# Where the third and fourth tile of the first expert's rows are turned

## The chip, the cores and the metric

The kernel runs on one core of a Trainium2 chip. A core has a matrix engine (TensorE, PE in the profile, with PEld for its weight loads), VectorE (DVE), ScalarE (ACT), GpSimd (POOL) and SyncE (SP), each with its own stream of instructions; DMA queues move data beside them. The metric is the device time of one execution in microseconds (us); the time of a kernel is the median of its runs. Names such as L1303 are lines of the kernel.

## The reference

Two layers, all in float32. First an attention with 4 batches, 8 heads, 768 tokens and head size 64, in which a token sees 8 global keys and the 96 keys up to itself. Its output, 3072 rows of 512, goes to a router: each row is given to the one of 8 experts whose embedding has the largest cosine with it, and is sent through that expert alone.

```
expert_idx = np.argmax(logits, axis=1)
for e in range(E):
    mask = expert_idx == e
    h = np.maximum(x[mask] @ w1[e], 0.0)        # w1[e]: 512 x 1024
    out[mask] = gate_w[mask, None] * (h @ w2[e])  # w2[e]: 1024 x 512
```

How many rows an expert gets depends on the data.

## The kernel before

**Attention** fills roughly the first 176 us. While it ends, the router writes for each row its number and gate to a list per expert in DRAM. The first 256 rows of expert 0 are taken early: they are gathered, turned and multiplied with expert 0's first weights before the lists are complete (L654 to L674). What remains of expert 0 and all rows of experts 1 to 7 come afterwards, in the loop at L1732.

**Widths.** An expert's rows are gathered in four tiles of 128 (512 at most). How many of them are real is known only on the chip. choose_widths (L1471) picks for each expert the smallest of a list of widths that holds its rows: for expert 0's remainder 128, 160, 192 and so on up to 512 (13 widths, L27), for the other experts 256 to 512. The products of an expert stand in a Switch with one arm for each width (L1375); PE and ACT, and from expert 1 on DVE too, jump to the arm that a register names. A hint about the jump is given ahead (give_hint, L1517); for expert 0 that is at L1716.

**Gathers.** gather_rows (L986) has POOL issue four indirect DMAs, one for each tile, into buffers xg (8 of them, so those of expert 0 are used again by expert 2). prepare (L1682) calls it one expert ahead.

**Turning.** The first products take the rows as columns of xT, so the gathered tiles (a row on each partition) must be transposed. turn_row (L1013) does that for one tile: four PE transposes into a PSUM tile "work" (three of them in turn), and two copies of 128x256 into xT, one for each half of the laced columns. The copies are done by the engine that is passed in.

```
for a in range(2):
    copy(out=xT[:, :, a, j * half : (j + 1) * half].rearrange(...), in_=laced(ps[:])[:, a])
```

xT holds all 512 columns, tile j in columns 64j to 64j+63 of each half. A product for width w reads columns 0 to w/2 - 1 of each half.

**Order around the change.** It is written by hand (a manual schedule on all engines); within one engine instructions run in the order of the program. From L1694 on:

- the lists' heads are loaded, cast to indices, and expert 0's four gathers are issued on POOL (L1706), then on SP the remaining pieces of expert 1's second weights, which wait for all four gathers (L1711 to L1714);
- pair.begin (L1718) multiplies the early 256 rows with the second weights, on PE;
- expert 0's four tiles are turned, with VectorE copying (L1721);
- VectorE casts the other experts' lists (L1723), splits them (L1724), clears the arms' result tiles (L1725) and makes sums of expert 1's first weights (L1728);
- the loop starts: POOL issues expert 1's gathers (L1739), and expert 0's Switch begins (L1375).

In an arm of expert 0, first_by_eight (L1273) multiplies the w columns of xT with the first weights in eight row blocks; ScalarE evicts each (L1281). After the row blocks 5, 6 and 7 the arm turns the tiles of expert 1 (between, L1355), with ScalarE copying. Then come the second products: part_in_arm (L1241) for a remainder of 32 or 64 rows and second_in_arm (L1232) for whole tiles beyond the first, and half of the first tile's product (L1390). Behind the arms follow the rest of it and the end of the early pair. At the loop's next turn POOL issues expert 2's gathers and then the scatters of expert 0's results (L1740); SP asks for expert 2's weights when the last of these scatters has landed (L1743).

For experts 1 to 7 the arms use first_by_seven (L1286), which saves one of eight block products by sums that VectorE makes; the tiles of an expert are turned in the arms of the expert ahead of it.

Of the kernel before, what the change touches and what calls it, by code (L numbers as in the profile page):

```python
# [20 lines left out]
P = 128  # L21
NEG = 1e9
CAP = 512
# [976 lines left out]
def new_turned(k):  # L1000
    return k.xtp.tile([P, k.NC, 2, CAP // 2], F32, name="xT", tag="xT")


def new_hidden(k):
    return k.hp.tile([P, k.NF, CAP], F32, name="hT", tag="hT")
# [80 lines left out]
def hidden_sums(k, a):  # L1086
    return left_sums(k, a, k.hsum)
# [258 lines left out]
def expert(k, now, coming, widths, unfinished):  # L1346


    tc = k.tc
    w1, w2 = now.w  # L1350
    hT = new_hidden(k)
    if coming:
        coming.xT = new_turned(k)

    def between(f):  # L1355
        at = {1: (0,), 2: (1,), 3: (2,), 4: (3,)} if now.e else {5: (0,), 6: (1, 2), 7: (3,)}
        for j in at.get(f, ()) if coming else ():
            turn_row(k, coming.rows, coming.xT, j, k.nc.scalar.copy)

    a = [[hT[:, 4 * j : 4 * j + 4, i * P : (i + 1) * P] for j in range(2)] for i in range(2)]  # L1360
    now.sums, spare = weight_sums(k, w2)
    left, making = hidden_sums(k, a)
    more, ahead = [], []
    if coming:
        coming.token_sums, more = token_sums(k, coming.xT)
        if now.e:
            coming.first_sums, ahead = first_sums(k, coming.w[0])
    spare = [spare[:2], spare[2:], ahead[:1], ahead[1:2], more[:2], []]
    if now.e == 1:
        spare[2:6] = [], ahead[:1], ahead[1:2] + more[:1], more[1:2]  # L1370
    tiles = range(2 if now.e else 1, CAP // P)
    ps = None if now.e else k.work0.tile([P, k.DM], F32, name="work", tag="work")
    k.order = list(range(4, 8)) + list(range(4)) if now.e else list(range(8))
    steps = widths_of(now.e)
    for arm in tc.Switch(now.width.index, len(steps), hint=now.width.hint):  # L1375
        w = steps[arm]
        if now.e:
            first_by_seven(k, now, hT, w, between, list(spare))
            for make in making:
                make()  # L1380
        else:
            first_by_eight(k, now.xT, w1, hT, w, between)
        for size in (32, 64):
            if w % (2 * size) >= size:
                part_in_arm(k, now, hT, w2, w // (2 * size) * 2 * size, size)
        for j in tiles:
            if j < w // P:
                second_in_arm(k, now, hT, w2, j)
        if ps:
            second(k, ps, hT, w2, range(k.NF // 2))  # L1390

    def scatters():
        for j in tiles:
            scatter_rows(k, now.y[:, j - 1, :], now.tile_ids[:, j : j + 1])
        for size in (64, 32):
            scatter_rows(k, now.y_part[size][:], now.parts[size][0], P // size)

    def choose_next():
        if coming:
            give_hint(k, coming.e, widths[coming.e])  # L1400

    out = [scatters]
    if now.e:
        pair = Pair(k, now.rows, a, left, w2, now.sums, not coming)
        choose_next()
        out += unfinished.pop()()
        number = [lambda: widths.append(take_width(k, now.e + 2))] if now.e + 2 < k.E else []
        if now.e == k.E - 2:
            number.append(lambda: load_flag(k))
        if now.e == 2:  # L1410
            ahead.append(lambda: flag_leftover(k))
        pair.begin(spare=(more[2:], number + ahead[2:3], ahead[3:]))
        ps = k.work0.tile([P, k.DM], F32, name="work", tag="work")
        unfinished.append(pair.end(ps[:, 0:256]))
        out.append(pair.scatter(1))
    else:
        choose_next()
        widths.append(take_width(k, 2))
        out += unfinished.pop()()
        for make in more:  # L1420
            make()
        second(k, ps, hT, w2, range(k.NF // 2, k.NF))
        unfinished.append(lambda: end_second(k, now.rows, ps))
    return out


def widths_of(e):
    return WIDTHS[PAIR:] if e else WIDTHS
# [168 lines left out]
def kernel(  # L1597
# [40 lines left out]
    with ExitStack() as moe:  # L1638
# [55 lines left out]
        with tc.manual_schedule(engines=ORDERED | set(ARMS) | {mybir.EngineType.Pool}):  # L1694
            choose_widths(n)
            sums, making = weight_sums(n, n.w[0][1])
            for make in making:
                make()
            numbers(0, 2)
            a = [[h[:, :, i * P : (i + 1) * P] for h in n.first.hT] for i in range(2)]  # L1700
            left, making = hidden_sums(n, a)
            making[1]()
            making[2]()
            making[0]()
            cast(0, 1)
            coming = prepare(0)  # L1706
            gathers = coming.gathers
            making[3]()
            cast(1, 2)
            numbers(2, n.E)  # L1710
            for e, i in n.weights:  # L1711
                part = load_weights_part(n, e, n.w[e], i)
                wait_for(n, part, gathers)
                gathers = []  # L1714
            widths = [take_width(n, 0), take_width(n, 1)]
            give_hint(n, 0, widths[0])  # L1716
            pair = Pair(n, n.first.rows, a, left, n.w[0][1], sums)
            pair.begin(True)  # L1718
            unfinished = [pair.end_apart]
            coming.xT = new_turned(n)  # L1720
            for j in range(CAP // P):  # L1721
                turn_row(n, coming.rows, coming.xT, j, nc.vector.tensor_copy)
            cast(2, n.E)  # L1723
            split_rows(n, n.mt)  # L1724
            for y, parts in ys:  # L1725
                for x in (y, *parts.values()):
                    nc.vector.memset(x[:], 0.0)
            first, making = first_sums(n, n.w[1][0])  # L1728
            for make in making:
                make()  # L1730
            pending = []
            for e in range(n.E):  # L1732
                now, coming = coming, None
                parts_of(n, now)
                now.width = widths[e]
                if e == 1:
                    now.first_sums = first
                if e + 1 < n.E:
                    coming = prepare(e + 1)  # L1739
                for scatter in pending:  # L1740
                    scatter()
                if e and coming:
                    wait_for(n, load_weights(n, e + 1, coming.w), [n.outs[-1] if e == 1 else n.out_again])  # L1743

                nc.gpsimd.drain()
                pending = expert(n, now, coming, widths, unfinished)
            for scatter in pending + unfinished.pop()():
                scatter()
# [31 lines left out]
```

## Time and profile before

| what | value |
|---|---|
| median of 3 runs | 523.97 us (522.73 to 524.47) |
| the profiled execution | 524.56 us |
| its span | 522.8 us |
| granted TensorE clock | 0.996 |
| PE idle between 200 us and its last matmul | 4.1 us in seven gaps over 0.1 us |
| expert 0's product, width 160 (L1279) | 209.75 to 220.0 us |

The profile is of one execution, and its span leaves out some 1.7 us around the program. In its timeline a line gives start, busy time, engine, line of the kernel, operation, tiles written and read, shape and number; in square brackets stands the idle time of that engine before it and what ended it. "issue" is time in which an engine waited for nothing that the profile shows. A chain of waits is followed back from the last instruction: at each step to what released it.

### The profile page before, as it was taken

The page shows a single profiled execution, that of the slowest core. Times are in us where ns is not written, and L with a number is a line of the kernel's source. Part 1 is how long each engine was busy: PE and PEld are TensorE (multiplying, and loading weights), DVE is VectorE, ACT ScalarE, POOL GpSimd, SP SyncE. Part 2 cuts the span into 40 slices and gives each one's busy share as a digit, 9 for nine tenths or more (in the row PEclk, how much of TensorE's full clock was granted, in tenths as well). Part 3 has the DMA queues.
Part 4 walks back from the last instruction along what each step waited for, and adds up shares of the span by engine and source line. Part 5 has one row for each costly group of instructions (what it writes and reads, how often), then busy time and mean ns, then how long its engine had stood idle before and what let it go on. Part 6 is the DMA issues. An engine that isn't in the chain of part 4 may idle for free.

```text
span 522.8 us, 13699 instructions
## 1 busy us (share of the span) xinstructions
PE 500.1 (96%) x5606; PEld 411.3 (79%) x5606; DVE 301.8 (58%) x602; ACT 197.2 (38%) x493; POOL 153.7 (29%) x169
## 2 busy tenths in 40 slices
PE   7899999999988998999999999999999999999995
PEld 7677887887765787859878759989889789859964
DVE  5647667666685664756745606765646644715531
ACT  4867766766653411302322312412312222302210
POOL 4221121442544235354240024144053050013023
PEclk9999999999998999999999999999999999999999
DMA  9999998898443346817573018357056064001001
GB/s 169 200 188 181 220 261 207 212 229 177 104 103 92 94 102 118 265 56 287 195 284 118 2 44 296 150 197 263 3 217 242 4 224 163 1 16 67 0 22 67
DMA packets 111421, 76.32 MB, mean 146 GB/s; under 512 B 87077, under 2 KB 95269, under 8 KB 111281
## 3 DMA queue, kind: packets, MB, share of 16 engines
q1 hardware_dynamic: 102769, 59.00, 42.1%
q0 software_dynamic: 6912, 15.26, 8.8%
q8 instruction: 63, 1.03, 0.9%
q14 instruction: 77, 0.63, 0.4%
q10 hardware_dynamic: 1600, 0.39, 0.3%
HBM read 61.66 MB, written 17.16 MB: 151 GB/s over the span
## 4 chain that ended last, share of the span: by engine, by line
PE 67%; issue 18%; DVE 3%; POOL 3%; ACT 3%; DMA 3%; SPq 1%; POOLq 1%; ACTq 0%; DVEq 0%
PE big L1303 17%; PE big L1108 9%; PE od L509 7%; PE pa L480 5%; PE work L1236 4%; PE od L519 3%; PE pa L455 3%; PE work L1108 3%; PE work L1249 3%; PE pa L671 2%; PE work L1017 2%; POOL out_dram L1255 2%; PE big L1279 2%; PE pa L582 2%; PE work L1027 1%
## 5 line engine op out<-in xcount | busy, mean ns | idle before, releaser
L493 DVE TENSOR_TENSOR ex<-ex,table 126x768 f32<-126x768 f32 x64 | 61.3, 964 | 45.1 <-ACT ex L486 44.9
L1315 DVE TENSOR_TENSOR hT<-big,hT 128x320 f32<-128x320 f32 (+4 forms) x70 | 39.4, 566 | 49.9 <-PE big L1303 49.7
L1255 POOL DMA_INDIRECT out_dram<-y_arm,tids x17 | 17.1, 1004 | 167.4 <-ACT y_arm L1238 121.1
L486 ACT ACTIVATE ex<-pa 126x384 f32<-126x384 f32 (+1 forms) x128 | 53.3, 477 | 24.4 <-PE pa L480 18.6
L1303 PE MATMUL big<-xT,w1t 128*128 128x160 f32 (+4 forms) x336 | 59.4, 330 | 1.1 <-issue 1.1
L1303 PEld LDWEIGHTS big<-xT,w1t 128*128 128x128 f32 x336 | 54.2, 190 | 3.9 <-issue 2.0
L991 POOL DMA_INDIRECT xg<-x_dram,idss x32 | 35.4, 1106 | 42.9 <-PE big L1303 21.5
L509 PE MATMUL od<-ex,v 126*64 126x192 f32 (+1 forms) x576 | 47.0, 309 | 0.0
L480 PE MATMUL pa<-qT,kT 64*32 64x128 f32 (+4 forms) x2048 | 41.0, 263 | 3.7 <-issue 3.5
L480 PEld LDWEIGHTS pa<-qT,kT 64*32 64x32 f32 (+1 forms) x2048 | 30.2, 105 | 16.7 <-issue 12.3
L257 POOL DMA_INDIRECT meta<-mt,slot x24 | 27.2, 1133 | 49.9 <-DVE rd L553 20.9
L509 PEld LDWEIGHTS od<-ex,v 126*64 126x64 f32 x576 | 35.3, 139 | 7.9 <-issue 3.8
L1303 PE MATMUL big<-xsum,fsum 128*128 128x160 f32 (+4 forms) x224 | 39.6, 330 | 0.0
L1020 ACT COPY xT<-work 128x256 f32<-128x256 f32 x56 | 18.1, 375 | 56.0 <-PE work L1017 55.3
L1303 PEld LDWEIGHTS big<-xsum,fsum 128*128 128x128 f32 x224 | 36.1, 190 | 1.2
L1236 PE MATMUL work<-w2t,hT 128*128 128x512 f32 x80 | 35.1, 594 | 0.0
L1108 PE MATMUL big<-wsum,hsum 128*128 128x256 f32 x136 | 31.1, 380 | 1.1 <-issue 0.6
L1317 ACT ACTIVATE hT<-hT 128x320 f32<-128x320 f32 (+4 forms) x42 | 21.6, 533 | 25.5 <-DVE hT L1315 25.3
L430 POOL COPY v<-v 30x896 f32<-30x896 f32 (+1 forms) x15 | 18.4, 1239 | 41.1 <-DMA v<-in_v_dram 28.9
L1108 PEld LDWEIGHTS big<-wsum,hsum 128*128 128x128 f32 x136 | 25.7, 190 | 5.6 <-issue 1.4
L1236 PEld LDWEIGHTS work<-w2t,hT 128*128 128x128 f32 x80 | 15.1, 190 | 17.7 <-issue 17.6
L1113 DVE TENSOR_TENSOR ptmp<-big,ptmp 128x256 f32<-128x256 f32 x16 | 6.7, 421 | 38.0 <-PE big L1108 20.0
(246 smaller groups left out, 899.8 us busy)
## 6 DMA issues: line engine op xcount, KB each, us to landing
w1t<-in_moe_w_dram SPq DMA_DIRECT2D x6, 2048.0 KB
w2t<-in_moe_w_dram SPq DMA_DIRECT2D x6, 2048.0 KB
v<-in_v_dram SPq DMA_DIRECT2D x32, 192.0 KB
x_dram<-xs SPq DMA_DIRECT2D x23, 256.0 KB
k<-in_k_dram SPq DMA_DIRECT2D x28, 192.0 KB
q<-in_q_dram SPq DMA_DIRECT2D x28, 192.0 KB
w1t<-in_moe_w_dram SPq DMA_DIRECT2D x32, 128.0 KB
w2t<-in_moe_w_dram SPq DMA_DIRECT2D x32, 128.0 KB
```

The lines of the kernel that those rows point to most:

```text
L257: i = nc.gpsimd.indirect_dma_start(out=k.meta[:], out_offset=bass.IndirectOffsetOnAxis(ap=slot[:, t : t + 1], axis=0), in_=mt[:, t, :], in ...
L480: i = nc.tensor.matmul(u.sp[e][k0:k1, a * n + c0 : a * n + c1], lhsT=t.kT[rows, j, k0:k1], rhs=t.qT[rows, j * BLK + c0 : j * BLK + c1], st ...
L486: nc.scalar.activation(u.ex[:, e], u.sp[e][0:ROWS, 0 : 2 * u.n].rearrange("p (a c) -> p a c", a=2), AF.Exp, scale=k.scale)
L493: nc.vector.tensor_tensor(out=exv, in0=exv, in1=tab[:, :, 0 : u.n // BLK, :], op=ALU.mult)
L509: nc.tensor.matmul(g.od[a][e * D : (e + 1) * D, at : at + c1 - c0], lhsT=g.v[0:ROWS, 2 * a + e, u.j, :], rhs=u.ex[:, e, a, c0:c1], start=f ...
L991: i = k.nc.gpsimd.indirect_dma_start(out=xg[:], out_offset=None, in_=k.x_dram[0 : upto or k.N + 1, :], in_offset=bass.IndirectOffsetOnAxis ...
L1108: i = self.k.nc.tensor.matmul(ps, lhsT=x[:, f, :], rhs=w[:, f, :], start=f == 0 and not add, stop=True, skip_group_check=True)
L1236: nc.tensor.matmul(ps[:], lhsT=hT[:, f, j * P : (j + 1) * P], rhs=w2[:, f, :], start=i == 0, stop=i == k.NF - 1)
L1255: i = k.nc.gpsimd.indirect_dma_start(out=k.out.rearrange("t (i m) -> (t i) m", i=n), out_offset=bass.IndirectOffsetOnAxis(ap=ids, axis=0), ...
L1303: nc.tensor.matmul(to[f // 2][:, f % 2 * 256 : f % 2 * 256 + h], lhsT=x[:, l, f * P : (f + 1) * P], rhs=y[:, l, 0:h], start=not (add or f ...
L1315: nc.vector.tensor_tensor(out=to, in0=x, in1=z, op=ALU.add)
L1317: nc.scalar.activation(to, to, AF.Relu)
```

## The change

Ahead of expert 0's Switch only the first two tiles are turned. In an arm, ahead of its products, those further tiles are turned that this arm's width reaches: none for widths up to 256, the third for 288 to 384, the third and fourth for 416 to 512. There ScalarE copies them, where VectorE did before. For the other experts turned_ahead gives 4, so the new loop has no turns. All four gathers are issued as before.

```diff
     for arm in tc.Switch(now.width.index, len(steps), hint=now.width.hint):
         w = steps[arm]
+        for j in range(turned_ahead(now.e), -(-w // P)):
+            turn_row(k, now.rows, now.xT, j, k.nc.scalar.copy)
         if now.e:
...
+def turned_ahead(e):
+    return CAP // P if e else 2
...
             coming.xT = new_turned(n)
-            for j in range(CAP // P):
+            for j in range(turned_ahead(0)):
                 turn_row(n, coming.rows, coming.xT, j, nc.vector.tensor_copy)
             cast(2, n.E)
```

## The prediction

> **What bounds the kernel now.** I read the page's busy shares and its chain first, then the chain and the timeline around the changed lines.
>
> ```profile
> PE 500.1 (96%) x5606; PEld 411.3 (79%) x5606; DVE 301.8 (58%) x602; ACT 197.2 (38%) x493; POOL 153.7 (29%) x169
> PE 67%; issue 18%; DVE 3%; POOL 3%; ACT 3%; DMA 3%; SPq 1%; POOLq 1%; ACTq 0%; DVEq 0%
> ```
>
> TensorE is the bound: 96% busy, and 67% of the chain. "DMA 3%" is small, but one piece of it lies exactly where the change works. The chain between 204 and 222 us:
>
> ```profile
> 204.00 4.61 DMA xg<-x_dram,idss
> 208.60 0.14 issue
> 208.74 0.63 PE work L1017 x4
> 209.36 0.39 issue
> 209.75 6.76 PE big L1279 x48
> ```
>
> Columns: start, duration, what. The gather of the fourth tile of expert 0's rows is issued at 204.00 and ends 4.61 us later. TensorE waits for it, turns that tile (four transposes, L1017), and only then begins expert 0's first product (L1279). The timeline of the same stretch, start and busy time first:
>
> ```profile
> 204.00 0.95 POOL L991 DMA_INDIRECT xg<-x_dram,idss  x1 [0.30 <-issue]
> 206.13 1.47 PE L1017 MATMUL work<-ident,xg 128*128 128x128 f32 x12
> 206.80 1.41 DVE L1020 COPY xT<-work 128x256 f32<-128x256 f32 x4
> 208.74 0.63 PE L1017 MATMUL work<-ident,xg 128*128 128x128 f32 x4 [1.13 <-DMA xg<-x_dram,idss]
> 209.75 6.76 PE L1279 MATMUL big<-xT,w1t 128*128 128x160 f32 x48 [0.39 <-issue]
> 210.02 0.76 DVE L1020 COPY xT<-work 128x256 f32<-128x256 f32 x2 [1.81 <-PE work L1017]
> 211.51 0.76 DVE L1020 COPY xT<-work 128x256 f32<-128x256 f32 x2 [0.73 <-PE big L1279]
> ```
>
> Twelve transposes (tiles 0 to 2) run without a gap, then TensorE idles 1.13 us for the DMA. The product's shape 128x160 tells which arm runs: width 160, which reads 160 columns, tiles 0 and 1 and no others. The last two rows are VectorE's copies of tiles 2 and 3; they start after the product has begun, so the product does not even wait for them.
>
> **The change part by part.** For width 160 the new loop in the arm is range(2, 2), so it is empty. In this run the work on tiles 2 and 3 is not moved, it disappears: eight transposes on PE, four copies on DVE.
>
> *PE, removed.* The third burst of four is a third of the run from 206.13 to 207.60: transposes start every 0.109 us, so 0.44 us. Then the wait, 1.13 us, and the last four transposes, 0.63 us. The 0.39 us of issue is the way into the Switch and stays. From the end of tile 1's transposes, 207.60 - 0.44 = 207.16, to the first product at 209.75 are 2.59 us.
>
> *What is late next.* The product needs both of tile 1's copies. They are in the row at 206.80: four copies in 1.41 us, to 208.21. I take 0.14 us from such an event to the first matmul (208.60 to 208.74 after the DMA): 208.21 + 0.14 = 208.35. The way into the Switch, 207.16 + 0.39 = 207.55, is hidden beneath the copies, with 0.80 us to spare. So the product starts at 208.35 and not at 209.75: **1.40 us earlier**. That is more than the bare wait of 1.13 and less than the 2.59 removed, because DVE's copies become the wait. Bounds: 2.20 us if the copies were not waited for (excluded: 32 columns of tile 1 are read), 0 if the wait for DVE took 1.40 longer than I think.
>
> *DVE.* Four copies at 0.417 us, 1.7 us, go, and the cast behind them (212.18) can start up to 4 us sooner. That is worth nothing on the path: the last of DVE's work there, expert 1's first sums (220.4 to 225.3), is read only from 237.1 on.
>
> *What must come as much earlier as PE.* The arm turns expert 1's rows after its sixth product; those transposes would move from 216.35, 217.88 and 219.84 to some 215.0, 216.5 and 218.4. The gathers for them are issued at 205.25 to 209.02; with the 4.61 us that expert 0's last gather took, the last lands at about 213.6. Cover: 4.8 us. ScalarE's evictions (L1281, 0.30 us each against 1.09 us of PE per row block) follow PE. From 235.3 on, stages show PE busy 32.86 of 34.00 and 247.66 of 248.70 us, so a shift at 210 us reaches the end; each expert's weights are released by PE's own progress (SP waits 137.5 us in five waits for "PE big L1108"), so the loads move with it.
>
> *Queues passed.* The gathers of tiles 2 and 3 are still issued, and the weight pieces on SP still wait for all four gathers: nothing moves there. POOL's gathers of expert 2 reuse the buffers of expert 0's tiles; for tiles 2 and 3 their last reader is now inside arms, some of which do not read them. The trace of before has no such release for these two. Lowest cost 0 (released at the arm's first instruction or before), highest as in the rival below. I take 0: these gathers start at 219.60, ten microseconds after the arm begins.
>
> *Code.* Eight transposes leave the common stream; eight wide arms that do not run here grow by four or eight transposes. Later code moves to other addresses. What a branch costs:
>
> ```profile
> L1775 PEldq COMPARE_BRANCH  x16: 295/314/3807, 209.0 to 499.3; - x16
> ```
>
> [...] Nearly all of it hides under matmuls already queued. The idle time of PE put to "issue" at the expert's ends is 0.55 us before L1108 at 228.15 and 1.14 us before L1303 at 269.27; the others are 0.3 us. Placing the code anew could remove these two (1.69 us) or lay bare a similar one elsewhere (+1.14). I take 0 for it, the trace having no sign which way.
>
> [...]
>
> *Sum.* 0.44 + 1.13 + 0.63 - 0.80 (new wait for the copies) = 1.40 us. The profiled execution took 524.56 us with a span of 522.8: the rest, 1.7 us, lies around it and stays, so it would take 523.16. The median of the runs is 0.59 below the profiled one; the same saving gives 523.97 - 1.40 = **522.6 us**.
>
> **The rivals.**
>
> *Faster still: code falls better.* The wait goes as above and the two bare "issue" gaps shrink as well. For it: they are tied to this layout. Against: nothing aims at them. 523.97 - 1.40 - 1.69 = 520.9 us.
>
> *No gain to speak of: a new wait in the old one's place.* PE now depends on a chain PE, DVE, PE just ahead of the product. The rows at 210.02 and 211.51 show that DVE may start late: tile 2's transposes ended at 207.60, and its copies started 2.4 us after that. Had tile 1's copies met such a delay, the product would start at 209.75 or later. Against: tiles 0 and 1 were copied without any gap. [...] 523.97 - 1.40 + 1.14 = 523.7 us.
>
> *Slower: the buffers come free too late.* If POOL may reuse the buffers of tiles 2 and 3 only when PE has left the arm and ended a product behind it (229.9 - 1.4 = 228.5), two gathers at 1.26 us come there, and POOL's scatters of expert 0's rows, begun now at 225.32, begin at 231.0 instead of 223.9: 7.1 us later. Expert 2's weights wait for the last of them (SP's longest wait for out_dram<-y,ids, 19.9 us), so they are asked for at 243.6 instead of 236.5. w1's 2.1 MB at the stage's 247 GB/s are 8.5 us, to 252; DVE reads them at 247.9 - 1.4 = 246.5, and behind that read stand the combinations that free PE's banks. PE would lose some 5 us less the 1.4 gained: 523.97 + 3.6 = 527.6 us. It decides only if the third gather waits more than 5 us: POOL idles 3.0 us between its gathers (end 222.35) and the first scatter, and the weights have about 2 us more. A branch into the arm that takes 3.4 us and no longer 0.39 (207.16 + 3.8 = 210.9) would also end above, at 525.1; but its hint is given at 195.0, 12 us ahead.
>
> *It does not do what it says* would be an arm other than 160; the shape 128x160 excludes that.
>
> **How the numbers follow.** Plain gain 0.62, better code 0.16, gain eaten 0.14, slower 0.08. About 0.3% (1.57 us) is what a measurement of this kernel can tell from no change. The plain gain, 1.40 us, lies just below it; with the small gaps of code and the scatter of the runs (522.73 to 524.47) I put 0.28 of its 0.62 beyond. Faster 0.28 + 0.16 = 0.44; same 0.34 + 0.14 = 0.48; slower 0.08. The range reaches from the better code (520.9) past the eaten gain (523.7) to the highest run shown, 524.5; the slower case and the tails stay out.
>
> **What would show it.** In the changed profile: eight transposes ahead of the product in place of sixteen, no wait for xg there, the product at about 208.35, DVE's copies at L1020 four in place of eight, L1279 again 128x160, the gathers of expert 2 near 218, the last pieces of the chain 1.4 us earlier. Wrong is the step on copies if the product starts behind 208.6; wrong is the step on the shift if the product starts at 208.35 and PE's last matmul does not end 1.4 us earlier; then the PE gaps at the joins tell where it went.

## The result, and the profile after

The kernel after took 525.68 us (median of 20 runs, 522.70 to 528.53). The kernel before, run beside it, took 526.41 us in 20 runs (522.11 to 529.37). The ratio is 0.9991, with an interval of 0.9971 to 1.0011: no difference that these runs can tell. The forecast, 522.6 us in a range of 520.9 to 524.5, lies 3.1 us too low. A few executions in the sets below were over 1.5% longer than the fastest of their kernel; the ratios and the differences at equal clock leave them out, the medians do not.

The first two lines are the busy times and the chain's shares on the page of the profiled execution of after (524.9 us, span 523.2).

```profile
PE 499.7 (96%) x5598; PEld 411.2 (79%) x5598; DVE 299.7 (57%) x598; ACT 197.0 (38%) x493; POOL 149.2 (29%) x169
PE 73%; issue 17%; ACT 4%; DVE 3%; POOL 2%; DMA 1%; POOLq 0%; DVEq 0%; ACTq 0%
```

Eight matmuls and four VectorE operations are gone, and the chain's DMA share fell from 3% to 1%. The chain of waits in the same stretch as before (start, duration, what):

```profile
203.79 4.75 PE big L1108 x22
208.54 0.89 PE work L1017 x8
209.43 0.02 issue
209.45 0.77 DVE xT L1020 x2
210.21 1.60 issue
211.81 6.76 PE big L1279 x48
```

No gather stands in it any more. In its place stand VectorE's copies and 1.60 us of "issue". The timeline (start, busy time, engine, line, operation; in brackets the idle time ahead) shows what that is:

```profile
208.38 1.04 PE L1017 MATMUL work<-ident,xg 128*128 128x128 f32 x8
209.45 0.76 DVE L1020 COPY xT<-work 128x256 f32<-128x256 f32 x2 [0.32 <-PE work L1017]
210.91 0.76 DVE L1020 COPY xT<-work 128x256 f32<-128x256 f32 x2 [0.70 <-PE work L1017]
211.81 6.76 PE L1279 MATMUL big<-xT,w1t 128*128 128x160 f32 x48 [2.40 <-issue]
```

TensorE ends the eight transposes at 209.42. VectorE is free at 210.21, yet it begins tile 1's copies only at 210.91: it is waiting for TensorE's signal that tile 1's transposes are done, and that signal comes 1.5 us after their end. (The ends of matmuls are modelled, so the profile cannot tell a late signal from transposes that really ended late; below both are called a late signal.) TensorE idles 2.40 us ahead of the first product. Before, it idled 1.52 us in two gaps and turned the two other tiles in the rest of that time.

**Where the time went, over all profiles.** The runs below gave several profiles of both kernels. I cut each at four points of the timeline: the first transpose of expert 0 (L1017), the first product of expert 0 (L1279), the first product of expert 1 (L1303's first), and the end of TensorE's last matmul. Times in us; an asterisk marks a stage in which TensorE ran at half clock for 3.41 us, which lengthens the first product by 1.7.

| profile | first transpose at | transpose to product | product to expert 1 | expert 1 to the end | gap before L1303 at expert 2 |
|---|---|---|---|---|---|
| before | 206.13 | 3.62 | 25.35 | 282.13 | 1.14 |
| before, e1 | 209.90 | 3.85 | 24.90 | 281.70 | 1.25 |
| before, e9 | 207.86 | 3.78 | 26.48* | 282.18 | 1.41 |
| after | 208.38 | 3.44 | 25.72 | 280.20 | none |
| after, e2 | 204.60 | 3.33 | 25.16 | 280.20 | none |
| after, e10 | 208.01 | 4.16 | 25.52* | 280.20 | none |
| after, e13 | 207.45 | 4.16 | 25.28* | 281.60 | 1.13 |

Three things can be read from it. At the place of the change nothing was gained on average: 3.75 us before (mean of three), 3.77 after (mean of four). Behind it, from expert 1 on, after is 1.45 us shorter on average (282.00 against 280.55), and that is the gap before L1303 at the way into expert 2's arm. And the start of the stage, in the second column, scatters over several microseconds, through code that is the same in both kernels. The fourth column differs by less than its scatter (means 25.58 and 25.42).

That gap in the timelines of before and then of after, TensorE alone:

```profile
266.24 1.89 PE L1108 MATMUL work<-w2t,hsum 128*128 128x256 f32 x8
269.27 3.04 PE L1303 MATMUL big<-xT,w1t 128*128 128x256 f32 x13 [1.14 <-issue]
```

```profile
268.66 1.89 PE L1108 MATMUL work<-w2t,hsum 128*128 128x256 f32 x8
270.39 1.89 PE L1303 MATMUL big<-xT,w1t 128*128 128x256 f32 x8
```

In the first, TensorE has nothing for 1.14 us; in the second, L1303 follows L1108 at once (consecutive groups overlap in these modelled ends). The branch ahead of it took 3397 ns in before and 404 ns in after.

### The profile page after: what moved, and what is told of

It reads as the page before. It is cut to its first block, busy times and chain, and to the rows that moved or that the text cites. A ratio compares the mean times of both kernels' runs of the same rounds, so it can differ in the third digit from the quotient of the medians.

```text
span 523.2 us, 13675 instructions
## 1 busy us (share of the span) xinstructions
PE 499.7 (96%) x5598; PEld 411.2 (79%) x5598; DVE 299.7 (57%) x598; ACT 197.0 (38%) x493; POOL 149.2 (29%) x169
## 4 chain that ended last, share of the span: by engine, by line
PE 73%; issue 17%; ACT 4%; DVE 3%; POOL 2%; DMA 1%; POOLq 0%; DVEq 0%; ACTq 0%
PE big L1303 17%; PE big L1108 11%; PE od L509 8%; PE pa L480 6%; PE work L1236 4%; PE od L519 4%; PE pa L455 3%; PE work L1108 3%; PE work L1249 3%; PE pa L671 3%; PE work L1017 2%; PE pa L582 2%; ACT ex L486 2%; POOL out_dram L1255 2%; PE big L1279 2%
## 5 line engine op out<-in xcount | busy, mean ns | idle before, releaser
L1303 PE MATMUL big<-xT,w1t 128*128 128x160 f32 (+4 forms) x336 | 59.3, 330 | 0.0
L1303 PEld LDWEIGHTS big<-xT,w1t 128*128 128x128 f32 x336 | 54.3, 190 | 2.4 <-issue 0.5
L480 PE MATMUL pa<-qT,kT 64*32 64x128 f32 (+4 forms) x2048 | 42.5, 263 | 5.7 <-issue 5.5
L991 POOL DMA_INDIRECT xg<-x_dram,idss x32 | 34.2, 1068 | 45.0 <-PE big L1303 19.2
L257 POOL DMA_INDIRECT meta<-mt,slot x24 | 26.1, 1087 | 49.6 <-DVE xs L591 10.5
L1303 PE MATMUL big<-xsum,fsum 128*128 128x160 f32 (+4 forms) x224 | 39.6, 330 | 0.0
L1303 PEld LDWEIGHTS big<-xsum,fsum 128*128 128x128 f32 x224 | 36.1, 190 | 1.2
L1108 PE MATMUL big<-wsum,hsum 128*128 128x256 f32 x136 | 31.1, 380 | 1.4 <-issue 0.9
L1108 PEld LDWEIGHTS big<-wsum,hsum 128*128 128x128 f32 x136 | 25.7, 190 | 6.0 <-issue 1.7
```

The costliest lines, as they stand in the source:

```text
L257: i = nc.gpsimd.indirect_dma_start(out=k.meta[:], out_offset=bass.IndirectOffsetOnAxis(ap=slot[:, t : t + 1], axis=0), in_=mt[:, t, :], in ...
L480: i = nc.tensor.matmul(u.sp[e][k0:k1, a * n + c0 : a * n + c1], lhsT=t.kT[rows, j, k0:k1], rhs=t.qT[rows, j * BLK + c0 : j * BLK + c1], st ...
L991: i = k.nc.gpsimd.indirect_dma_start(out=xg[:], out_offset=None, in_=k.x_dram[0 : upto or k.N + 1, :], in_offset=bass.IndirectOffsetOnAxis ...
L1108: i = self.k.nc.tensor.matmul(ps, lhsT=x[:, f, :], rhs=w[:, f, :], start=f == 0 and not add, stop=True, skip_group_check=True)
L1303: nc.tensor.matmul(to[f // 2][:, f % 2 * 256 : f % 2 * 256 + h], lhsT=x[:, l, f * P : (f + 1) * P], rhs=y[:, l, 0:h], start=not (add or f ...
```

## The experiments

Eighteen runs were made, in four sets; some repeat a kernel. Each set ran beside the kernel before on one chip: e1 to e4 on one, e5 to e8 on another, e9 to e12 on a third, e13 to e18 on that of e5 again at a later time (e16 to e18 eight minutes after e13 to e15, with no profile of after beside them). **Equal clock** below means this: each run lists its mean granted TensorE clock, and in every set the time falls as the clock rises, by 0.34 to 0.56 us per 0.001 (520 us times 0.001 is 0.52). One slope in common for a set, fitted by least squares over its runs, takes that part out; what is left of the difference to before is given with its standard error. The clock is itself a result of a run, so the ratio as measured stands beside it.

### First set: is it noise, and what holds the copies back?

**e1**, the kernel before as it is.

> The kernel before, unchanged, for the noise of times and the spread of single profiles. Read are three stretches: the start up to the first transpose of expert 0's rows (206.13 us in the profile of before, 208.38 in that of after, though the code up to there is the same), from the first transpose to the first product of expert 0 (3.62 before, 3.43 after), and from that product to TensorE's last matmul (307.49 before, 305.92 after). Theory S (the first stretch scatters by itself): it moves by 1 us or more against 206.13 here too, while the second stays within 0.2 of 3.62. Rival (a kernel's stages are fixed, so the 2.25 us of the first stretch are the change's own): 206.1 within 0.3. Ratio 1.000 with an interval of about 0.2% either way.

Measured: 525.88 us, ratio 0.9998 (0.9971 to 1.0025); at equal clock -0.16 +- 0.44 us.

**e2**, the kernel after as it is.

> The changed kernel, unchanged. Theory L (TensorE's last completion signals ahead of the jump into the arm reach VectorE late, so that the copies of tile 1 end some 3.3 us after the first transpose and the new wait eats the gain): first transpose to first product again 3.2 to 3.6 us. Rival A (that profile was an accident): 2.2 us, as predicted. Third stretch 305.9 again if it belongs to the layout of the code, 307.5 if the 1.6 us are scatter. Ratio 0.997 to 1.001.

Measured: 524.10 us, ratio 0.9967 (0.9937 to 0.9998); at equal clock -2.82 +- 0.45 us. The first product came 3.33 us after the first transpose: tile 1's copies were late again, by as much as in the first profile of after.

**e3**, three tiles turned ahead.

```diff
 def turned_ahead(e):
-    return CAP // P if e else 2
+    return CAP // P if e else 3
```

> Three tiles are turned ahead of the Switch, the fourth in the arms that read it, so there is no wait for the fourth gather, and tile 2's transposes stand between tile 1's and the jump. Theory L (the signals just ahead of the jump are late, whichever tile they belong to): the copies of tiles 0 and 1 come on time, as in the kernel before, and the first product starts 2.2 to 2.4 us after the first transpose; tile 2's copies come late and nobody waits. Rival T (the signals are late at this time because of the traffic of the gathers, wherever the jump is): 3.2 to 3.6 us, as in the changed kernel. Time under L 1.2 us less than before (ratio 0.998), under T as the changed kernel.

Measured: 523.59 us, ratio 0.9946 (0.9916 to 0.9976), at equal clock -1.92 +- 0.44. Tile 1's copies began 2.37 us after the first transpose although four more transposes stood behind tile 1's, and the product came at 3.27. So in this profile the signal is not late because a jump follows it: that theory falls. The gap before L1303 was there, 1.15 us.

**e4**, VectorE and ScalarE take one of each tile's two copies.

```diff
-def turn_row(k, rows, xT, j, copy):
+def turn_row(k, rows, xT, j, copy, other=None):
...
-        copy(out=xT[...
+        (other if a and other else copy)(out=xT[...
...
-                turn_row(n, coming.rows, coming.xT, j, nc.vector.tensor_copy)
+                turn_row(n, coming.rows, coming.xT, j, nc.vector.tensor_copy, nc.scalar.copy)
```

> The changed kernel, with each tile's second copy done by ScalarE, idle there, in place of VectorE, so that both copies of a tile run side by side. Theory L (the late signal is the wait): tile 1's signal comes 2.5 us after the first transpose as in the changed kernel, one copy of 0.4 us in place of two in a row of 0.77 behind it, and the product starts at about 3.1 us. If the copies' own length is the wait (the prediction's step): 1.04 for the transposes, 0.42 for the copies and 0.14, so 1.6 us. Time 0.3 to 0.4 us less than the changed kernel under L, 0.6 less under the other.

Measured: 523.14 us, ratio 0.9946 (0.9918 to 0.9974), at equal clock -2.65 +- 0.46. Product at 2.00, where theory L had 3.1 and the other 1.6: the signal of tile 1 was on time in this profile (VectorE began its copy at 1.07), but ScalarE's copies waited for VectorE's and the last began at 1.53. Gap before L1303: 1.09 us.

What follows: in this set the kernels with fewer turns ahead are some 2 to 3 us faster at equal clock (e2, e3, e4 against e1), though the first 20 runs of either kernel showed no difference; and in e2 and e3 the gain does not lie where the forecast had it.

### Second set: the code, and the traffic

**e5**, no executed instruction changed, only addresses. To the kernel before, the wide arms of expert 0 get the turns that the change puts there; all four tiles are still turned ahead.

```diff
         w = steps[arm]
+        for j in range(CAP // P if now.e else 2, -(-w // P)):
+            turn_row(k, now.rows, now.xT, j, k.nc.scalar.copy)
```

> The kernel before, with all four tiles turned ahead as it had them; only the wide arms, which do not run here, get the turns of tiles 2 and 3 that the change puts there (written a second time, to no effect). So no executed instruction differs from the kernel before, only the addresses behind the first expert's arms move. Theory K (the 1.14 us gap of PE before L1303 and its 3.2 to 3.6 us branch are a matter of where the code lies): the stretch from the first product to PE's last matmul leaves the 306.6 to 307.5 us of the two profiles of before, and if the gap happens to close it is 305.4 to 305.9, with a branch of about 0.4 us there; if the address falls badly too, it is unchanged or another gap shows. Rival N (the gap closed because the product began earlier, or because VectorE and POOL had less to do): gap of 1.1 us and 306.6 to 307.5, as before. Both: 3.6 to 3.9 us from the first transpose to the first product.

Measured: 519.86 us beside 519.80, ratio 0.9995 (0.9965 to 1.0025), at equal clock -0.18 +- 0.46. The gap before L1303 is gone and its branch took 409 ns. But the way out of expert 1's arm, where before, e1 and e9 show no gap, now shows one:

```profile
251.79 1.13 PE L1108 MATMUL big<-w2t,hT 128*128 128x256 f32 x4
253.94 1.02 PE L1108 MATMUL big<-w2t,hT 128*128 128x256 f32 x4 [1.01 <-issue]
```

So in this profile, with only the addresses moved, one gap is closed and another of nearly the same size stands elsewhere. Net: nothing.

**e6**, the kernel after without the turns in the wide arms.

```diff
-        for j in range(turned_ahead(now.e), -(-w // P)):
-            turn_row(k, now.rows, now.xT, j, k.nc.scalar.copy)
```

> The kernel after without the turns of tiles 2 and 3 in the wide arms (left out: what those arms would turn; the arm that runs here reads neither tile). Every executed instruction is that of the kernel after, the code behind the first expert lies lower. Theory K: the gap of 1.1 us before L1303 can come back, with a branch of 3.2 to 3.6 us, and the stretch from the first product to PE's last matmul goes from 305.4-305.9 back to about 307. Rival N: no gap, 305.4 to 305.9 as after. Both: 3.3 to 3.5 us from the first transpose to the first product.

Measured: 514.94 us beside 519.80 (six runs), ratio 0.9907 (0.9878 to 0.9936), at equal clock -3.64 +- 0.61. No gap before L1303, against what theory K allowed. And here is the forecast's own stretch as the forecast had it:

```profile
200.75 1.04 PE L1017 MATMUL work<-ident,xg 128*128 128x128 f32 x8
201.42 1.40 DVE L1020 COPY xT<-work 128x256 f32<-128x256 f32 x4
202.97 1.32 PE L1279 MATMUL big<-xT,w1t 128*128 128x160 f32 x8 [1.19 <-DVE idss L1684]
```

The four copies run on without a gap, and the product comes 202.97 - 200.75 = 2.22 us after the first transpose. The forecast had 208.35 - 206.13 = 2.22. The stretch ahead of it executes what after executes; only TensorE's signals came on time. (The release is put down to a later VectorE operation, the cast at L1684; it is the copies' end, 202.82, that the product waited for.)

**e7**, no gather in flight while tiles 0 and 1 are turned.

```diff
-            xgs, t.gathers = gather_rows(n, n.ids[:, e], n.xgp)
+            xgs, t.gathers = gather_rows(n, n.ids[:, e], n.xgp, CAP // P if e else 2)
+            if e == 1:
+                for x in t.gathers:
+                    wait_for_it(n, x, turned[-1])
+            xgs = xgs if e else xgs * 2
...
-                wait_for(n, part, gathers)
+                wait_for(n, part, turned[-1:])
```

> The kernel after with no gather in flight while the first two tiles are turned: the first expert's third and fourth gather are left out (their rows are never read here), and the second expert's four gathers and the pieces of its weights wait for VectorE's copy of the second tile. Theory T (TensorE's signals come late while gathers are under way): tile 1's copies start 1.05 to 1.4 us after the first transpose and the first product 2.0 to 2.3 us after it. Rival P (the lateness belongs to TensorE's own stream at this place, whatever the traffic): copies at 2.4 us, product at 3.3 to 3.5. The whole time will be longer in both cases, since the second expert's rows and weights are asked for later.

Measured: one run, 518.37 us. Product at 2.23. It tells nothing by itself, since e5, e6 and e8 had their signals on time too in this set.

**e8**, e3 and e4 together.

> Three tiles turned ahead, and each tile's two copies shared by VectorE and ScalarE. Theory S2 (two engines halve the copies; the signal's lateness is a matter of luck): the first product comes 2.0 to 3.0 us after the first transpose, 0.4 us below what one engine gives with the same signals; a signal at 2.4 gives copies to 2.85 and the product at 3.0. Rival (two waiting engines get the signal on time): 2.0 us again, as in the run with two tiles and two copiers. Time: 0.3 to 1.3 us below the kernel after if its code has no bare wait, and as much as 1.1 more with it.

Measured: 516.59 us beside 519.80, ratio 0.9951 (0.9928 to 0.9973), at equal clock -2.11 +- 0.47. Product at 2.00, gap before L1303 1.53 us.

### Third set: before and after side by side, once more

**e9**, **e10**, **e11** and **e12** are the kernels of e1, e2, e6 and e4 again.

> The kernel before, once more, for a profile of it on the same chip as the three runs that follow, and for the noise. Two theories of what the change brings meet here. Theory 1 (the sum of the forecast, 1.40 us at the way into the first product, plus 1.1 us for the bare wait before L1303): this profile shows 3.6 to 3.9 us from the first transpose to the first product and a gap of 1.0 to 1.25 us before L1303. Against the kernel before: 0, within 0.7 us.

Measured: 527.05 us, ratio 1.0000 (0.9971 to 1.0029), at equal clock -0.25 +- 0.47. Product at 3.78, gap 1.41.

> The kernel after, once more, beside before on the same chip. Theory 1: if tile 1's copies start on time (about 1.1 to 1.35 us after the first transpose, as in the run of the kernel without the arms' turns), the first product comes 2.2 us after the first transpose, 1.4 to 1.6 less than before; with the late start seen twice (2.4 to 2.5) it comes at 3.3 to 3.45. No gap before L1303. So at equal granted clock it is 2.5 to 3 us faster with signals on time, 1.5 to 2 with late ones. Rival 2 (the change is worth nothing): 0, within 0.7 us at equal clock.

Measured: 527.24 us, ratio 0.9988 (0.9951 to 1.0024), at equal clock -2.33 +- 0.50. Product at 4.16: later than in any profile of before. No gap before L1303. Rival 2 falls at equal clock, but not in the ratio as measured: the runs of after had a lower mean clock, 0.9918 against 0.9950 (in the first set 0.9954 against 0.9965).

The profile of e10 (mean clock 0.993) shows a stretch of lower clock. Busy time by windows of its timeline: length, then PE, PEld, DVE, ACT, POOL, then PE's granted clock, the DMA share and GB/s.

```profile
208.00:212.10 4.10, 1.05 (x9) 0.80 (x7) 2.08 (x7) 0.00 (x0) 2.91 (x4) 1.00 0.79 231
212.10:216.10 4.00, 3.94 (x17) 3.97 (x18) 3.53 (x24) 0.30 (x1) 0.00 (x0) 0.57 0.85 240
216.10:220.00 3.90, 3.90 (x31) 3.90 (x30) 3.29 (x5) 1.21 (x4) 0.60 (x1) 1.00 0.85 266
```

TensorE is nearly idle up to 212.1 and then has only 0.57 of its clock for 4 us: 17 matmuls where the next window of nearly the same length has 31. In the records of the clock this is one window of 3.41 us at half clock, and the product's 48 matmuls take 8.43 us and not 6.76.

> The kernel after without the turns in the wide arms (left out: what those arms, which do not run here, would turn), once more. Before, it stood 4.9 us below the kernel before in its six undisturbed runs. Theory 1: it executes what the kernel after executes, so at equal granted clock it stands with the kernel after within 0.7 us, unless a bare code wait differs, and each such wait is seen in its profile. Rival 3 (leaving out the arms' turns is worth something by itself, about 1 us or more): it is faster than the kernel after though no PE gap differs.

Measured: 526.31 us, ratio 0.9985 (0.9950 to 1.0021), at equal clock -2.59 +- 0.51, so with after (-2.33): rival 3 falls. Product at 3.44 this time, with a half-clock window behind it. No gap before L1303. The profile of e6 had signals on time, no half-clock window and no gap before L1303 (the bare code wait of the expectation) together; that these three made up its 4.9 us is likely, but no run took them apart.

> The kernel after with each tile's two copies shared by VectorE and ScalarE, once more. On-time signals: first product 2.0 us after the first transpose, only 0.2 less than with one engine; late signals: 2.8 to 3.0. Its bare wait before L1303 (1.09 us) stays, since the code lies as it did: so it is 0.5 to 1 us slower than the kernel after, at equal clock, with signals on time, and about equal with late ones.

Measured: 524.78 us, ratio 0.9960 (0.9932 to 0.9987), at equal clock -3.53 +- 0.47. Product at 2.06, and no gap before L1303 (branch 403 ns), though the code is that of e4, which had 1.09. So the addresses within the program do not settle the gap alone. The expectation that it would be slower than after is refuted. Its stretch, with one of tile 1's copies on each engine:

```profile
205.82 1.04 PE L1017 MATMUL work<-ident,xg 128*128 128x128 f32 x8
206.50 0.88 DVE L1020 COPY xT<-work 128x256 f32<-128x256 f32 x2
206.94 0.84 ACT L1020 COPY xT<-work 128x256 f32<-128x256 f32 x2 [1.68 <-DVE xT L1020]
207.88 1.32 PE L1279 MATMUL big<-xT,w1t 128*128 128x160 f32 x8 [1.02 <-DVE xT L1020]
```

### Fourth set: one cause or two, and where the lateness comes from

**e13** is the kernel after, **e14** and **e16** that of e7, one run each.

> The kernel after, for its profile beside the next two on one chip. With late signals: tile 1's copies 2.4 to 3.3 us after the first transpose, first product at 3.3 to 4.2. With signals on time: copies at 1.3, product at 2.2. No gap before L1303 in both cases.

Measured: 525.98 us; product at 4.16. Contrary to the expectation the gap before L1303 was there, 1.13 us, with a branch of 3293 ns: the kernel after can meet it too.

> The kernel after with no gather in flight while tiles 0 and 1 are turned (the first expert's third and fourth gather left out, the second expert's gathers and weight pieces held until the copies of tile 1), once more. If the kernel after shows late signals in this same job: theory T (the gathers make TensorE's signals late) expects copies of tile 1 at 1.05 to 1.4 us and the first product at 2.0 to 2.3; rival P (the lateness has another source) expects 2.4 or later, and 3.3 or later. If the kernel after shows none, this run tells nothing on that.

Measured: 523.76 us; product at 2.23, in the same set in which after had 4.16.

**e15**, the kernel before without the wait for the third and fourth gather.

```diff
             coming.xT = new_turned(n)
+            first_two = (None, None, coming.rows[2][:2] * 2)
             for j in range(CAP // P):
-                turn_row(n, coming.rows, coming.xT, j, nc.vector.tensor_copy)
+                turn_row(n, first_two, coming.xT, j, nc.vector.tensor_copy)
```

> The kernel before with all its sixteen transposes and eight copies ahead of the Switch, but the third and fourth turn read the rows of tiles 0 and 1 and not those of the third and fourth gather (left out: the true rows of these two tiles, which the arm that runs here does not read). Code and instructions are those of before; only the wait for the two gathers is gone. Theory 1 (two separate effects): the first product moves up by what the change alone moves it, to 2.2 to 2.5 us behind the first transpose with signals on time and 3.3 with late ones, and the gap of 1.1 to 1.4 us before L1303 stays, with 306.6 to 307.5 us from the first product to PE's last matmul at full clock. At equal clock it is 0.3 (late signals) to 1.4 us (on time) faster than before, so 1 to 2 us short of the kernel after. Rival N (the gap closes because the product begins earlier): no gap, and as fast as the kernel after, 2.4 to 2.8 us below before.

Measured: 526.48 us beside 528.08, ratio 1.0006 (0.9972 to 1.0040), at equal clock -0.17 +- 0.65. Product at 2.48, so 1.3 us earlier than the mean of before, which the time alone does not show; and the gap stays:

```profile
266.09 1.89 PE L1108 MATMUL work<-w2t,hsum 128*128 128x256 f32 x8
269.42 1.75 PE L1303 MATMUL big<-xT,w1t 128*128 128x256 f32 x7 [1.44 <-issue]
```

An earlier product does not close it, and the time is not the 2.4 to 2.8 us below before that rival N expects: rival N falls, the two are separate effects. With before's code (e15's but for the waits) the gap has now been there in four profiles of four, with after's in one of four.

**e17** and **e18** are e7 with the weight pieces waiting for the two gathers only, so that they move during the turns.

```diff
-                wait_for(n, part, turned[-1:])
+                wait_for(n, part, gathers)
```

> The kernel after with neither gathers nor weight pieces in flight while tiles 0 and 1 are turned (the first expert's third and fourth gather left out), a third look. Theory T (gathers under way make TensorE's signals late): copies of tile 1 at 1.33 us behind the first transpose, first product at 2.2. Rival P (late in about half of all profiles, whatever moves): late with a chance of a half, copies at 2.4 or later, product at 3.3 or later.

> The same without the gathers (the first expert's third and fourth left out, the second expert's held until the copies of tile 1), but the pieces of the second expert's weights wait only for the first two gathers, so that they move while tiles 0 and 1 are turned. Theory T (gathers): product at 2.2 us behind the first transpose. Theory T2 (any heavy transfer makes the signals late): copies at 2.4 or later and product at 3.3 or later, at least in one of the two looks. Rival P: late with a chance of a half.

> The kernel of the run before, a second look, with the same expectations: 2.2 us under theory T, 3.3 or later under T2 in at least one of the two, one or the other by chance under rival P.

Measured: 526.80, 522.97 and 521.59 us, and the product at 2.23 in all three. Without gathers in flight tile 1's signals were on time in five profiles of five; with them, late in eight of fifteen. Were the gathers of no account, five of five would come by chance in some 5% of cases (792 of 15504 ways), if each profile stands for itself. Theory T stands, but it is not shown. T2 finds no support: weight pieces that moved during the turns (237 GB/s from 208 to 210 us in e17) delayed nothing in two runs.

Four things in the traces bear on theory T. First, the gathers are not enough: in all fifteen profiles POOL issues the next three at the same places, 0.4, 1.6 and 2.9 us behind the first transpose, whether the signals are late or on time. Second, taking the gathers away also took POOL's issuing away, and no run separates the two. Third, the second set differs from the others in its record: the traces of e5, e6 and e8 hold 81 to 89 semaphore updates in the 5 us behind the first transpose, those of the twelve other profiles with gathers only 15 to 19, so there most updates were not recorded. All eight late signals are among these twelve, and so are all stalls of the small matmuls shown further down; the three complete records have none. Whatever keeps the updates from the record, the recording itself included, is thus a rival that stands untested. Lastly, with two copiers (e4, e8, e12) tile 1's signal was on time in three profiles of three; that too could be chance.

## Why the prediction was wrong

**The work removed: right.** Eight transposes in place of sixteen, no wait for the gathers, arm 160. The 2.20 us of PE work and waiting left the chain.

**The new wait for the copies: the step that failed.** The prediction put it at 0.80 us, from "What is late next": copies end at 208.21, product at 208.35. The arithmetic holds to a hundredth where TensorE's signals are on time (2.22 to 2.23 us in e6, e7, e14, e16, e17 and e18). Wrong was that they would be. In the four profiles of after, tile 1's copies began at 2.5, 2.4, 3.3 and 3.3 us behind the first transpose and not at 1.3, and the wait grew from 0.80 to between 1.9 and 2.7 us. The prediction's own second rival had this mechanism, "VectorE may start late", with the right row beside it (tile 2's copies, 2.4 us late). It was weighed at 0.14 because tiles 0 and 1 had been copied without a gap in the one profile at hand. In e1 and e9, the same kernel, tile 1's copies were late too, at 2.45 and 2.51. Nobody waited for them there: the fourth gather ended later still. The wait that went had covered one that was already there. Why the signals are late stays open, as said under e18.

**The shift reaches the end: wrong for the stretch up to 224 us, right behind it.** In after there was no shift to pass on. Where the product did come early, part of it was lost in the second products of the same arm, 64 small matmuls at L1249. First before, then e12, then e6:

```profile
220.37 1.39 PE L1249 MATMUL work<-w2t,hT 128*32 128x128 f32 x28
222.06 0.43 PE L1249 MATMUL work<-w2t,hT 128*32 128x128 f32 x4 [0.30 <-issue]
222.80 1.17 PE L1249 MATMUL work<-w2t,hT 128*32 128x128 f32 x32 [0.31 <-issue]
```

```profile
218.49 1.88 PE L1249 MATMUL work<-w2t,hT 128*32 128x128 f32 x46
220.71 0.39 PE L1249 MATMUL work<-w2t,hT 128*32 128x128 f32 x2 [0.33 <-issue]
221.46 0.38 PE L1249 MATMUL work<-w2t,hT 128*32 128x128 f32 x3 [0.36 <-issue]
222.21 0.27 PE L1249 MATMUL work<-w2t,hT 128*32 128x128 f32 x1 [0.37 <-issue]
222.90 0.65 PE L1249 MATMUL work<-w2t,hT 128*32 128x128 f32 x12 [0.42 <-issue]
```

```profile
213.58 1.95 PE L1249 MATMUL work<-w2t,hT 128*32 128x128 f32 x64
```

In e6 they run on; in the others they come in small groups with waits that the profile puts to "issue". The next table has profiles without a half-clock window; the starts are in us behind the first transpose.

| profile | first product | L1249 takes | next product (L1027) |
|---|---|---|---|
| before | 3.62 | 3.53 | 17.76 |
| before, e1 | 3.85 | 3.87 | 18.33 |
| after | 3.44 | 3.56 | 17.61 |
| after, e2 | 3.33 | 3.59 | 17.54 |
| e3 | 3.27 | 3.77 | 17.65 |
| e15 | 2.48 | 4.04 | 17.13 |
| e12 | 2.06 | 4.99 | 17.66 |
| e4 | 2.00 | 4.77 | 17.39 |
| e6 | 2.22 | 1.88 | 14.72 |
| e8 | 2.00 | 1.88 | 14.60 |

The product of e4, e12 and e15 came 1.55 us earlier than that of before and e1, L1027 only 0.65. The prediction named the gaps ("the others are 0.3 us"), but its check of the shift began at 235.3; from 221.0 to 235.3 TensorE had been busy 13.04 of 14.30 us. What holds these matmuls up is not shown. Behind it the step holds: from expert 1's first product to the end the time is 280.20 us, to a hundredth, in the three profiles of after without that gap and also in e6, e11 and e12.

**Code, taken as 0: the second term that was mis-sized.** It measured -1.45 us on average (282.00 to 280.55 us), near the bound of -1.69, though all of it at one of the two gaps that make up that bound. That this is the change's doing is likely but not shown: a gap in four profiles of four with before's code against one of four with after's comes by chance in 5 of 70 cases, and e3, e4 and e8, all made from after, have the gap too. The branch durations go with it; the row below is that of the Switch in after (minimum, median, longest in ns).

```profile
L1781 PEldq COMPARE_BRANCH  x16: 294/396/3746, 208.0 to 499.8; - x16
```

The range is that of before, 295 to 3807: branches as long remain, hidden under queued matmuls (in after 3640 ns at 232.22 and 3746 ns at 499.76, with TensorE busy throughout). The one into expert 2's arm took 3.4 to 3.8 us in the three profiles of before and 0.40 in three of the four of after. In every profile where it is short, a fetch of 16 KB on queue q8 begins 2.6 to 6.7 us ahead of the branch (2.65 in after, for 404 ns); in every one where it is long, the fetch begins 0.6 to 1.1 us after the branch has (0.90 in before, for 3397 ns). The expectations call the gap behind a long branch a bare code wait; that such a branch waits for its code was an estimate and is not shown: the profile does not say which code a fetch brings, and the longest branch of before, 3807 ns at 229.81, has fetches 5.53 and 2.44 us ahead of it too. The 1.14 us that the rival of the eaten gain adds is the gap of before, taken once more; no profile shown here has a second such gap beside the first, and in e5 one of 1.01 us stood in its place. What brings the fetch ahead of the branch in one load of the same program and not in another (e4 and e12, after and e13) stays open.

**VectorE, ScalarE, buffers: right.** The rival on buffers falls: expert 2's gathers begin 7.3 us behind expert 0's first product in before (217.09 - 209.75) and in after (219.12 - 211.81), released by TensorE's turning in both.

**The base: wrong from the start.** 523.97 us was the median of three runs; twenty gave 526.41. The first transpose begins anywhere from 199.9 to 209.9 us in nineteen profiles (at 212.2 in that of e4, an execution 5.8 us above its kernel's median), behind code that is the same in all of them up to there, but for some gathers left out or held in e7, e14 and e16 to e18, which lie well inside these ends. The lowest four, 199.9 to 202.3, are those of the second set, where before took 519.80 us and not 525.8 to 528.1 as in the others. A range of 3.6 us around three runs could not hold that. The prediction is off by 3.1 us; some 2.4 of these are the base.

**Two rivals at once.** "No gain, a new wait in the old one's place" happened at the way into the product, "code falls better" behind it. The list had them as alternatives. By the stages of the profiles the two come to 0.0 and -1.45 us; at equal clock after stands at -2.82 +- 0.45 and -2.33 +- 0.50, some 1 us or two to three standard errors more, which is not accounted for; as measured, the ratios are 0.9991, 0.9967 and 0.9988.

**What stays open.** Whether the change lowers TensorE's clock. In the ten profiles where TensorE idles 1.5 us or more between first transpose and product, five show a half-clock window of 3.41 us that begins 0.3 to 1.4 us into the product; in the ten with 1.2 us or less, none. After belongs to the first kind, with 2.3 to 3.1 us idle, but so does before with its 1.5 to 1.7: the profiles show no difference between these two. The mean clocks of the runs point both ways: against before, after has -0.0011 +- 0.0011 (standard error) in e2 and -0.0031 +- 0.0010 in e10; its like without the wide arms' turns has -0.0030 +- 0.0013 in e11 and +0.0023 +- 0.0010 in e6.

**Perhaps a better version** is that of e4 and e12, with two copiers: ratios 0.9946 (0.9918 to 0.9974) and 0.9960 (0.9932 to 0.9987) to before, where after had 0.9967 and 0.9988 beside them. It idles only 1.0 us ahead of the product. The intervals overlap those of after, so that it is faster than after is not shown.

## What to carry to other kernels

When a wait goes, look for what it covered: a later waiter may have been late all along, and a row nearby that is late "where it does not matter" is the best evidence for that. A chain of PE, another engine, and PE again just ahead of a long stretch needs a price for a late signal (here 1.1 to 1.9 us on top of the 0.8). Follow a shift through every stage behind the change: one between the change and the first stage that was checked gave part of it back. And before a saving of a microsecond is forecast on a kernel that is disturbed by several, take the scatter of the base from where it arises, and not from three runs.

## What the runs showed of the hardware

**Late signals.** The signal that tile 1's transposes were done reached VectorE 1.3 to 2.2 us after their modelled end in 8 of 15 profiles with gathers under way, all 8 among the 12 whose record of semaphore updates is incomplete there; without gathers in 0 of 5.

**A half-clock window.** Five profiles have one at the first product (e5, e9, e10, e11 and e13). It lasts 3.41 us each time, and the product's 48 matmuls take 8.43 us and not 6.76, 1.7 us more. In each of the five TensorE had idled 1.5 to 3.1 us between the first transpose and the product. Idle time alone does not settle it: e5 has 1.52 us of it within 3.79 us and a window, before has 1.52 us within 3.62 us and none.

**A long branch.** The branch into expert 2's arm takes 404 ns of TensorE's queue in after, where a fetch of 16 KB on q8 begins 2.65 us ahead of it, and 3397 ns in before, where the fetch begins 0.90 us after it has begun; over the profiles of before and after it is 0.4 or 3.3 to 3.8 us. The long one lays bare 1.09 (e4) to 1.53 us (e8) of TensorE, 1.14 in before, the rest being hidden under queued matmuls.
